# Value products of 64 columns placed before 64-column low products, and a head's first scores joined with the last head's smallest transposes

## The chip, the cores and the metric

The kernel runs on one core of a Trainium2 chip. The metric is the device time of one execution in microseconds. Of the kernel before there are three timed runs: median 1168.77 us, 1167.53 to 1171.01. A profiled execution gives the trace, from which all durations below are taken.

## The reference

Attention with a decay from the cumulated logarithm of gates, causal, over 8 batches of 8 heads with 576 tokens and 64 values a head; then a feed-forward layer with softplus over all 4608 tokens.

```python
scores = scale * np.matmul(q, k.transpose(0, 1, 3, 2))
cum = np.cumsum(np.log(np.clip(f, 0.0001, 1.0)), axis=-1)
decay = cum[:, :, :, None] - cum[:, :, None, :]
scores = np.where(causal, -1000000000.0, scores + decay)
attn = np.exp(scores - np.max(scores, axis=-1, keepdims=True))
attn = attn / (np.sum(attn, axis=-1, keepdims=True) + 1e-09)
x = np.matmul(attn, v)            # heads put side by side: 4608 x 512
h = x @ w_in                      # 512 -> 2048
g = np.maximum(h, 0.0) + np.log1p(np.exp(-np.abs(h)))
out = g @ w_out                   # 2048 -> 512
```

## The kernel before

Products are made in a rounded 32-bit format whose operands are split into a high and a low part: `x` becomes `xh` and `xl`, and a product is the sum of high times high, low times high and high times low. So most matrices appear twice in the code, with h and l at the end of their names.

*Jobs.* Batch 0 is cut into smaller jobs, made without the split (`plain`). The other 56 heads are "whole" heads: jobs made by `whole`, worked by the functions inside `attention`. A whole head has five query tiles: 64 queries, then four times 128. Each tile's scores against all keys up to its end are two products into one PSUM bank (`scores`, lines 799 and 800); the last tile, 576 keys wide, takes two banks. VectorE adds the mask and takes the row minimum (line 804), ScalarE makes the exponential with the row sum (line 832). When all tiles of the head are done, `finish_stats` makes reciprocals, and each tile is scaled by them (line 862 or 860, on POOL, VectorE or ScalarE).

*Transposes.* `weights(bi)` transposes the scaled weights of four "banks" of keys into PSUM (`turn`, line 927), and splits them into high (line 216, a copying helper, or 946) and low (949). Bank 0 is the small one: the first 64 keys for the first 64 queries, and the last 64 keys for the last 64 queries. It has 64 rows only, so high and low lie one above the other in one tile `ph`, and one product takes both. Its transposes have 64 stationary columns. Banks 1 to 3 are 512, 448 and 320 + 192 columns wide.

*Values.* `output(gi)` (line 1060) multiplies: the stationary operand is `vhl`, the high and low values of a chunk of keys side by side, 2 x 64 = 128 columns; the moving one is `ph` or `pl`. The upper 64 rows of the result are what the high values give, the lower 64 what the low values give; `shift` copies one half to `x`, `put` (line 1086) adds the other. Group 0 is the first 64 queries, one product of 64 columns. Group 1 is the other 512 queries: 512 columns high and low, the other 64-column product, 448 high and low, 320 high and low, 192 high and low. Each group has a PSUM bank of its own.

*Feed-forward.* Blocks of 512 tokens: products up (line 1210, twelve for each 128 of the 2048), gate, products down (line 1295). Their units are dealt out between the units of the heads, so that TensorE has them to do while a head waits.

*Order.* The program's text makes no order of its own. Every step is an `Op` with its engines' estimated costs, the steps it comes after and the PSUM or SBUF buffers that it takes (`takes`); `Plan.run` plays these through and gives out, at each point, the step that could start first, ties by its place in the list. The engines' instruction streams are what comes out. A step that takes PSUM banks of tag "att" (four banks) must be first in that tag's queue; a `loose` step may pass others if one more bank than it needs is free. Scores are loose. `on_pe` is the estimate of a product: 0.444 ns a moving column, but no less than 0.92 ns a stationary column, so 0.12 us for 64 columns against 128.

*The loop over jobs* (line 1549 and what follows) makes the list: for job n the scores of head n (`s_`) and the transposes and value products of head n - 1 (`w_`, `o_`), as: tiles 0, 1, 2; banks 0 and 1; tile 3; bank 2; group 0 of the output; bank 3; preparation of the next head; tile 4; group 1; `finish_stats`.

Of the kernel before, what the change touches and what calls it, by code (L numbers as in the profile page):

```python
# [157 lines left out]
def on_pe(n, times=1, m=128):  # L158

    return On("PE", times * (max(n * 0.000444, m * 0.00092) + 0.002))  # L160
# [7 lines left out]
def on_turn(n):  # L168

    return On("PE", 0.109 * n)  # L170
# [49 lines left out]
def tile_decay_attention_softplus_ffn(  # L220
# [18 lines left out]
    B, D, H, _, S = qkT.shape  # L239
# [20 lines left out]
                x32=2, wl=2, vhl=3, vraw=1, raw=2, one=2)  # L260
    plan = Plan(BUFS | dict(T0=4, stat=4, p=2, xh0=1, xh1=1, xl0=1))
    add, give = plan.add, plan.give

    def add_dma(emit, kb, n=1, eng="SP", **more):
        return add(on_dma(kb, n, eng), emit, lag=dma_lag(kb, n, eng), **more)
# [6 lines left out]
    def bank(tag, name):  # L272
        return psum.tile([P, 512], F32, tag=tag, name=name, bufs=BUFS[tag])
# [12 lines left out]
    T = {}  # L286
# [321 lines left out]
    def attention(job):  # L608
# [161 lines left out]
            st["T"] = [a, q0_]  # L770


        def stat_tile(ti):
            q0, n_q, k0, pi, po = tiles[ti]
            end = q0 + n_q
            if ti == 0:
                st["p"] = add(NO_ENGINE, mark, takes=("p",), lag=0.0)
            m1, s1 = nm[0:n_q, ti : ti + 1], ls[0:n_q, ti : ti + 1]
            m0, s0 = nm[0:n_q, 5:6], lp[0:n_q, 4:5]
            if end - k0 <= 512:  # L780
                pieces = [(k0, end, s1)]
            else:
                mid = (k0 + end) // 2
                pieces = [(k0, mid, s0), (mid, end, s1)]
            todo, mins = [], []
            for i, (a, z, acc) in enumerate(pieces):
                box = {}
                final = z == end

                def scores(e, box=box, a=a, z=z):  # L790
                    o = bank("att", f"s{n}_{ti}_{a}")[:, 0 : z - a]
                    box["o"] = o[0:n_q]
                    if plain:
                        e.matmul(  # L794
                            o, part32(0, q0, q0 + P), part32(1, a, z), start=True, stop=not quad,
                        )
                        return
                    o = box["o"]
                    e.matmul(o, qA[:, q0:end], kA[:, a:z], start=True, stop=False)  # L799
                    e.matmul(o, qB[0:ST, q0:end], kB[0:ST, a:z], start=False, stop=True)  # L800

                def row_min(e, box=box, w=z - a, i=i, final=final):
                    right = MW - P + n_q if final else w
                    e.tensor_tensor_reduce(  # L804
                        out=box["o"], in0=box["o"], in1=cmask[0:n_q, right - w : right],
                        scale=-0.125, scalar=m0 if i else 3.0e38, op0=ALU.add, op1=ALU.min,
                        accum_out=m1 if final else m0,
                    )

                def sums(e, box=box, h=heads[ti % len(heads)]):  # L810
                    c, (plus, minus) = cum[0][:, 0:P], (x[:, h : h + 1].to_broadcast([BH, P]) for x in eye8)
                    e.matmul(box["o"], c, plus, start=False, stop=False)
                    e.matmul(box["o"], minus, c, start=False, stop=True)

                on = on_pe32(z - a) if plain else on_pe(z - a, 2)
                o = add(on, scores, after=st["T"], takes=("att",), loose=True)
                if quad:
                    o = add(on_pe32(2 * P), sums, after=[o, decay_ready["quad"]] + eye8_set)
                    cum_used.append(o)
                m = add(  # L820
                    On("DVE", 0.076 + (z - a) / 960), row_min, lag=0.2, after=[o] + mask_set + stat_set,
                    takes=("stat",) if ti == 0 and i == 0 else (),
                )
                st.setdefault("scores", []).append(o)
                st.setdefault("min", []).append(m)
                mins.append(m)
                todo.append((a, z, acc, box))
            for a, z, acc, box in todo:

                def weight(e, a=a, z=z, box=box, acc=acc):  # L830
                    o = pt[pi][0:n_q, po + a - k0 : po + z - k0]
                    e.activation(o, box["o"], AF.Exp, bias=m1, scale=-1.0, accum_out=acc)  # L832

                x = add(on_act(z - a, 0.19, True), weight, after=mins + [st["p"], ps_set[number % 2, pi]])
                give("att", [x])
                st.setdefault("sum", []).append(x)
                st.setdefault("exp", {}).setdefault(ti, []).append(x)
# [31 lines left out]
        used = {i: [] for i in range(len(banks))}  # L869
        tags = {}  # L870

        def weights(bi):
            spans, w = [], 0
            for key, lo, hi, vi, vc in banks[bi]:
                spans.append((key, lo, hi, (vi, vc), w))
# [73 lines left out]
                e.tensor_sub(box["l"], box["ps"][:, 0:w], box["h"].bitcast(F32))  # L949

            need = list(dict.fromkeys(need)) + halves_set
            m = add(on_turn(len(blocks) - 0.48 * small + len(sums)), turn, after=need, takes=("att",))
            for _ in spread_:
                give("one", [m])
            st.setdefault("turned", []).append(m)
# [87 lines left out]
            for bi, ops in used.items():  # L1043
                give(tags[bi], ops)

        def output(gi):
            g0, g1, h, tok = groups[gi]
            g, j = h // 2, h % 2
            todo = sorted(
                (p for p in parts if p[0] < g1 and p[1] > g0), key=lambda p: (max(p[0], g0) > g0, p[2])  # L1050
            )
            box, last = {}, []
            for i, (lo, hi, bi, vc, at, pbox, ready, small) in enumerate(todo):
                a, z = max(lo, g0), min(hi, g1)

                def values(e, i=i, a=a, z=z, vc=vc, o=at + a - lo, pbox=pbox, xs="h" if small else "hl"):
                    if i == 0:
                        box["ps"] = bank("att", f"o{n}_{gi}")
                    for x in xs:
                        e.matmul(  # L1060
                            box["ps"][:, a - g0 : z - g0], st["vhl"][:, vc[1], :],
                            pbox[x][:, o : o + z - a],
                            start=i == 0 and x == "h", stop=i == len(todo) - 1 and x == xs[-1],
                        )

                on = on_pe(z - a, len("h" if small else "hl"))
                op = add(
                    on, values, after=ready + last + st["V"],
                    takes=("att",) if i == 0 else (),
                )  # L1070
                last = [op]
                used[bi].append(op)
            st.setdefault("ends", []).extend(last)
            w = g1 - g0


            def to():
                if b not in x_of:
                    x_of[b] = buf("x32", [P, NCC, S], f"x32_{b}")
                return x_of[b][64 * j : 64 * j + 64, g, tok : tok + w]  # L1080

            def shift(e):
                copy(e, to(), box["ps"][64 - 64 * j : 128 - 64 * j, 0:w])

            def put(e):
                e.tensor_add(to(), box["ps"][64 * j : 64 * j + 64, 0:w], to())

            needs = last + x_taken.get(b, [])
            takes = () if b in x_taken else ("x32",)
            c = add(on_act(w, psum=True), shift, after=needs, takes=takes)  # L1090
            d = add(on_dve(w), put, after=[c])
            x_taken.setdefault(b, [c])
            puts = [d]
            wrote.setdefault(b, []).append((tok, tok + w, d))
            give("att", puts)
            if gi == len(groups) - 1:
                give("T", st["scores"])
                give("vhl", st["ends"])
                for bi, ops in used.items():
                    if banks[bi][0][:3] == (0, 0, 64):  # L1100
                        give("ph64", ops)
                    else:
                        give("ph", ops)
                        give("pl", ops)

        def loads():
            if quad:
# [7 lines left out]

        return dict(
            load=loads, prepare=None if plain else prepare, fin=finish_stats,
            s=[lambda ti=ti: stat_tile(ti) for ti in range(nt)],
            w=[lambda bi=bi: weights(bi) for bi in range(len(banks))],
            o=[output_tiled] if plain else [lambda gi=gi: output(gi) for gi in range(len(groups))],  # L1120
        )


# [414 lines left out]
    for n in range(len(jobs) + 1):  # L1538
# [10 lines left out]
        s_, w_, o_ = list(cur["s"]), list(old["w"]), list(old["o"])  # L1549
        units = s_[:-2] if len(s_) > 3 else s_[:1]  # L1550
        s_ = s_[len(units) :]
        if w_:
            for i, u in enumerate(w_[:-1]):
                units.append(u)
                if i == 1 and s_:
                    units.append(s_.pop(0))
            if len(o_) > 1:
                units.append(o_.pop(0))
            units.append(w_[-1])
# [68 lines left out]
```

## Time and profile before

| | |
|---|---|
| median of three runs | 1168.77 us |
| the profiled execution's own time | 1169.16 us |
| its span, from first to last instruction | 1167.4 us |
| products on TensorE | 6236 |
| first and last scores of a whole head | 113.0 and 959.4 us |
| DMA, share of 16 engines | 54% |

In rows of the trace, PE is TensorE's products and PEld its loads of stationary operands, which run beside products; DVE is VectorE, ACT ScalarE, POOL GpSimd. `o<-ph,vhl 128*128 128x64` reads: tile `o` is written from `ph` and `vhl`, the stationary operand has 128 rows and 128 columns, the moving one 128 rows and 64 columns. In grouped rows stand the busy time, the mean length of one in ns, then the engine's idle time just before and who ended it. In rows in order of time stand start and length in us. Ends of products are modelled, so recorded products overlap; what a product costs TensorE is read from start to start.

### The profile page before, as it was taken

How to read it: one execution, taken by the hardware profiler on the slowest of the kernel's cores; microseconds unless marked ns; L12 is line 12 of the kernel's file. 1: busy time of each engine (PE TensorE's matmuls, PEld its weight loads, DVE VectorE, ACT ScalarE, POOL GpSimd, SP SyncE). 2: the span in 40 equal slices, each digit the busy share in tenths (PEclk: the TensorE clock that was granted, in tenths of full speed). 3: DMA queues.
4: the chain of work that ended last, by engine and by line, in shares of the span. 5: the costliest groups of instructions: out<-in, count | busy, mean ns of one | idle time of the engine just before them, and what ended most of it. 6: DMA issues, size and time to landing. Idle time of an engine off the chain costs nothing.

```text
span 1167.4 us, 19457 instructions
## 1 busy us (share of the span) xinstructions
PE 1153.1 (99%) x6236; PEld 958.0 (82%) x6236; DVE 799.1 (68%) x1986; ACT 834.1 (71%) x1987; POOL 146.1 (13%) x158
## 2 busy tenths in 40 slices
PE   8999999999999999999999999999999999999998
PEld 6776788888888888888888888888888888888887
DVE  7889999877776778667877777677866772223322
ACT  6887788978867877678767786787867873444543
POOL 3424221100111101011011001110011100000000
PEclk9999999999999999999999999999999999999999
DMA  8867776555666546656566557654666433211211
GB/s 240 245 211 212 193 187 164 144 153 164 160 195 183 155 133 199 180 156 170 152 173 185 161 152 202 175 153 141 188 169 185 121 110 124 75 54 37 90 55 37
DMA packets 118758, 180.36 MB, mean 155 GB/s; under 512 B 20784, under 2 KB 78416, under 8 KB 118656
## 3 DMA queue, kind: packets, MB, share of 16 engines
q1 hardware_dynamic: 118488, 178.97, 53.7%
q8 instruction: 50, 0.82, 0.3%
q14 instruction: 52, 0.43, 0.1%
q10 hardware_dynamic: 168, 0.15, 0.0%
HBM read 109.98 MB, written 35.95 MB: 125 GB/s over the span
## 4 chain that ended last, share of the span: by engine, by line
PE 85%; DVE 8%; DMA 3%; ACT 2%; issue 1%; SPq 0%; POOL 0%; DVEq 0%; ACTq 0%; POOLq 0%
PE acc L1295 30%; PE h L1210 30%; PE b L927 7%; PE o L1060 6%; PE s L800 3%; PE s L799 3%; DMA T<-T 2%; PE h L1191 1%; DVE s L804 1%; PE s L794 1%; PE acc L1314 1%; ACT p L832 1%; DMA wl<-wil_d 1%; DVE xl L1162 1%; DVE pl L949 1%
## 5 line engine op out<-in xcount | busy, mean ns | idle before, releaser
L1210 PE MATMUL h<-xh,wih 128*128 128x512 f32 (+1 forms) x576 | 230.4, 403 | 0.0
L832 ACT ACTIVATE p<-s,negm 128x288 f32<-128x288 f32 (+7 forms) x384 | 183.6, 481 | 57.2 <-DVE negm L804 52.4
L1210 PE MATMUL h<-xl,wih 128*128 128x512 f32 (+1 forms) x576 | 216.6, 379 | 0.0
L804 DVE CUSTOM_DVE_ANT_0 s<-s,cmask 128x288 f32<-128x288 f32 (+6 forms) x320 | 137.9, 440 | 88.5 <-PE s L800 83.4
L862 POOL TENSOR_SCALAR p<-p,rsum 128x448 f32<-128x448 f32 (+4 forms) x89 | 98.8, 1119 | 744.1 <-DVE rsum L846 390.0
L1257 DVE SCALAR_TENSOR_TENSOR h<-h,e 128x512 f32<-128x512 f32 x136 | 95.8, 705 | 130.5 <-ACT e L1249 129.4
L1243 ACT ACTIVATE e<-h 128x512 f32<-128x512 f32 x144 | 85.9, 597 | 118.2 <-PE h L1210 117.1
L1295 PE MATMUL acc<-woh_dt_float32r,gh 128*128 128x512 f32 x376 | 152.8, 406 | 0.0
L1210 PE MATMUL h<-xh,wl 128*128 128x512 f32 (+1 forms) x576 | 148.8, 380 | 0.0
L1295 PE MATMUL acc<-woh_dt_float32r,gl 128*128 128x512 f32 x376 | 147.2, 391 | 0.0
L1295 PE MATMUL acc<-wol_dt_float32r,gh 128*128 128x512 f32 x376 | 147.0, 391 | 0.0
L949 DVE TENSOR_TENSOR pl<-b,ph 128x512 fp32r<-128x512 f32 x168 | 111.1, 666 | 32.2 <-ACT ph L216 28.9
L216 ACT CAST ph<-b 128x512 fp32r<-128x512 f32 (+2 forms) x178 | 85.3, 483 | 58.2 <-PE b L927 52.6
L1210 PEld LDWEIGHTS h<-xh,wl 128*128 128x128 f32 x576 | 104.8, 188 | 21.6
L927 PE MATMUL b<-ident,p 128*128 128x128 f32 (+1 forms) x728 | 118.8, 269 | 2.5 <-ACT p L832 1.2
L1265 DVE TENSOR_TENSOR gl<-h,gh 128x512 fp32r<-128x512 f32 x136 | 93.6, 688 | 40.4 <-ACT gh L216 39.9
L1210 PEld LDWEIGHTS h<-xh,wih 128*128 128x128 f32 x576 | 108.7, 189 | 15.2 <-issue 0.2
L1210 PEld LDWEIGHTS h<-xl,wih 128*128 128x128 f32 x576 | 108.9, 189 | 14.4 <-DVE xl L1162 0.2
L927 PEld LDWEIGHTS b<-ident,p 128*128 128x128 f32 (+1 forms) x728 | 86.6, 138 | 18.3 <-ACT p L832 3.9
L216 ACT CAST gh<-h 128x512 fp32r<-128x512 f32 x114 | 67.0, 588 | 46.9 <-DVE h L1257 43.3
L799 PE MATMUL s<-T 128*64 128x64 f32 x336 | 98.0, 303 | 0.9 <-ACT p L832 0.6
L800 PE MATMUL s<-T 68*64 68x64 f32 x336 | 97.7, 295 | 0.0
(166 smaller groups left out, 2218.9 us busy)
## 6 DMA issues: line engine op xcount, KB each, us to landing
wl<-wil_d SPq DMA_DIRECT2D x72, 512.0 KB
T<-T SPq DMA_DIRECT2D x224, 144.0 KB
raw<-in_qkT SPq DMA_DIRECT2D x112, 144.0 KB
g_d<-gh SPq DMA_DIRECT2D x84, 128.0 KB
g_d<-gl SPq DMA_DIRECT2D x84, 128.0 KB
vr<-in_vR SPq DMA_DIRECT2D x64, 160.0 KB
out<-ob SPq DMA_DIRECT2D x35, 256.0 KB
sto<-in_w_out SPq DMA_DIRECT2D x11, 512.0 KB
```

The lines of the kernel that those rows point to most:

```text
L216: (e.tensor_copy if hasattr(e, "tensor_copy") else e.copy)(out, in_)
L799: e.matmul(o, qA[:, q0:end], kA[:, a:z], start=True, stop=False)
L800: e.matmul(o, qB[0:ST, q0:end], kB[0:ST, a:z], start=False, stop=True)
L804: e.tensor_tensor_reduce(out=box["o"], in0=box["o"], in1=cmask[0:n_q, right - w : right], scale=-0.125, scalar=m0 if i else 3.0e38, op0=AL ...
L832: e.activation(o, box["o"], AF.Exp, bias=m1, scale=-1.0, accum_out=acc)
L862: e.tensor_scalar(a, a, f_, None, ALU.mult)
L927: e.transpose(box["ps"][0 : x.shape[1], at : at + one.shape[1]], x, one)
L949: e.tensor_sub(box["l"], box["ps"][:, 0:w], box["h"].bitcast(F32))
L1210: e.matmul(o, l, r, start=m == 0, stop=m == 11)
L1257: e.scalar_tensor_tensor(h, h, 0.0, box["e"], ALU.max, ALU.add)
L1265: e.tensor_sub(box["l"], box["t"], box["h"].bitcast(F32))
L1295: e.matmul(st["acc", tt], l, r[fc], start=first and m == 0, stop=last and m == 2,)
```

## The change

The two groups of the output become one chain. `output()` goes through the four wide parts of group 1 (512, 448, 320, 192 columns), each high and then low. Between the high and the low product of the second part it puts the 64-column product of group 0, between those of the third part the 64-column product of group 1. The low product behind a 64-column one then has only the high values as its stationary operand, 64 columns (`m`), and writes only the upper 64 rows: low weights times low values are left out there. The other two low products keep 128 columns. The chain takes group 1's bank with its first step and group 0's with its second, and stands where group 1 stood; `finish` holds the shift and the addition as before, group 0 first.

`joined` and `join` put several steps' instructions into one `Op` with the sum of their costs and all that they come after. For whole heads with a whole head before them, tile 0's scores (two products of 64 columns) and bank 0's transposes become such a joined item: it stands after tiles 1 and 2 where bank 0 stood, takes two PSUM banks at once, and isn't loose. The buffers that tile 0 took for the head are taken by whichever tile comes first.

```diff
+    def join(op, cost, emit, after):
+        op.parts.append(emit)
+        op.on = [On("PE", op.on[0].cost + cost)]
+        for d in after:
+            if d not in op.after and d is not op:
+                op.after.append(d)
+                d.users.append(op)
+                op.missing += 1
+        return op
...
-                o = add(on, scores, after=st["T"], takes=("att",), loose=True)
+                if into:
+                    o = join(into, 0.106, scores, st["T"])
+                else:
+                    o = add(on, scores, after=st["T"], takes=("att",), loose=True)
...
+            if into:
+                m = join(into, 0.164, turn, need)
+            else:
+                m = add(on_turn(len(blocks) - 0.48 * small + len(sums)), turn, after=need, takes=("att",))
...
+            wide = sorted((x for x in todo if not x[-1]), key=lambda x: x[1])
+            narrow = sorted((x for x in todo if x[-1]), key=lambda x: x[0])
+            last, done = [], {}
+            for i, part in enumerate(wide):
+                mine = [part] + narrow[i - 1 : i] * (0 < i <= len(narrow))
+                fresh = [x[0] for x in mine if x[0] not in done]
...
+                    def product(x, which, m=2 * D):
+                        gi, a, z, _, c, o, pbox, *_ = x
                         e.matmul(
+                            boxes[gi]["ps"][0:m, a:z], st["vhl"][:, c, 0:m], pbox[which][:, o : o + z - a],
...
+                    for x in mine:
+                        product(x, "h")
+                    product(mine[0], "l", D if len(mine) > 1 else 2 * D)
...
+                    On("PE", on_pe(w, 2).cost + 0.054 * (len(mine) - 1)), values,
+                    after=list(dict.fromkeys(r for x in mine for r in x[7])) + last + st["V"],
+                    takes=("att",) * len(fresh),
...
+        if nplain < n < len(jobs):
+
+            def row(s=units.pop(0), w=w_[0]):
+                op = joined()
+                s(op)
+                w(op)
+                op.takes = "att", "att"
+                plan.queue["att"].append(op)
+
+            w_[0] = row
```

More of the change, by code (lines that the diff above doesn't have):

```diff
@@ L262, in tile_decay_attention_softplus_ffn, with joined, row @@
     add, give = plan.add, plan.give
+    def joined():
+        parts = []
+        def row(e):
+            for part in parts:
+                part(e)
+        op = add(On("PE", 0.0), row)
+        op.parts = parts
+        return op
[7 more added lines that the diff above has]
+                op.missing += 1
+        return op
     def add_dma(emit, kb, n=1, eng="SP", **more):
@@ L770, in prepare, with stat_tile @@
             st["T"] = [a, q0_]
-        def stat_tile(ti):
+        def stat_tile(ti, into=None):
             q0, n_q, k0, pi, po = tiles[ti]
             end = q0 + n_q
-            if ti == 0:
+            if "p" not in st:
                 st["p"] = add(NO_ENGINE, mark, takes=("p",), lag=0.0)
@@ L821, in stat_tile @@
                     On("DVE", 0.076 + (z - a) / 960), row_min, lag=0.2, after=[o] + mask_set + stat_set,
-                    takes=("stat",) if ti == 0 and i == 0 else (),
+                    takes=() if "stat" in st else ("stat",),
                 )
+                st["stat"] = True
                 st.setdefault("scores", []).append(o)
@@ L870, in attention, with weights @@
         tags = {}
-        def weights(bi):
+        def weights(bi, into=None):
             spans, w = [], 0
@@ L951, in weights @@
             need = list(dict.fromkeys(need)) + halves_set
-            m = add(on_turn(len(blocks) - 0.48 * small + len(sums)), turn, after=need, takes=("att",))
+            if into:
+                m = join(into, 0.164, turn, need)
+            else:
+                m = add(on_turn(len(blocks) - 0.48 * small + len(sums)), turn, after=need, takes=("att",))
             for _ in spread_:
@@ L1044, in output_tiled, with output, values @@
                 give(tags[bi], ops)
[L1046 to L1059, printed above, removed]
+        def output():
+            boxes = [{} for _ in groups]
+            todo = []
+            for gi, (g0, g1, *_) in enumerate(groups):
+                for lo, hi, bi, vc, at, pbox, ready, small in parts:
+                    a, z = max(lo, g0), min(hi, g1)
+                    if a < z:
+                        todo.append((gi, a - g0, z - g0, bi, vc[1], at + a - lo, pbox, ready, small))
+            wide = sorted((x for x in todo if not x[-1]), key=lambda x: x[1])
[4 more added lines that the diff above has]
+                fresh = [x[0] for x in mine if x[0] not in done]
+                def values(e, i=i, mine=mine, fresh=fresh):
+                    for gi in fresh:
+                        boxes[gi]["ps"] = bank("att", f"o{n}_{gi}")
+                    def product(x, which, m=2 * D):
+                        gi, a, z, _, c, o, pbox, *_ = x
@@ L1060, in values @@
                         e.matmul(
-                            box["ps"][:, a - g0 : z - g0], st["vhl"][:, vc[1], :],
-                            pbox[x][:, o : o + z - a],
-                            start=i == 0 and x == "h", stop=i == len(todo) - 1 and x == xs[-1],
-                        )
-                on = on_pe(z - a, len("h" if small else "hl"))
+                            boxes[gi]["ps"][0:m, a:z], st["vhl"][:, c, 0:m], pbox[which][:, o : o + z - a],
+                            start=gi in fresh and which == "h",
@@ L1067, in output @@
+                            stop=gi == 0 or (i == len(wide) - 1 and which == "l"),
+                        )
+                    for x in mine:
+                        product(x, "h")
+                    product(mine[0], "l", D if len(mine) > 1 else 2 * D)
+                w = part[2] - part[1]
                 op = add(
-                    on, values, after=ready + last + st["V"],
-                    takes=("att",) if i == 0 else (),
+                    On("PE", on_pe(w, 2).cost + 0.054 * (len(mine) - 1)), values,
+                    after=list(dict.fromkeys(r for x in mine for r in x[7])) + last + st["V"],
+                    takes=("att",) * len(fresh),
@@ L1070, in output @@
                 )
                 last = [op]
-                used[bi].append(op)
-            st.setdefault("ends", []).extend(last)
-            w = g1 - g0
+                for x in mine:
+                    used[x[3]].append(op)
+                    done[x[0]] = [op]
+            for gi, (g0, g1, h, tok) in enumerate(groups):
+                finish(gi, h // 2, h % 2, g1 - g0, tok, boxes[gi], done[gi])
+            give("T", st["scores"])
+            give("vhl", last)
+            for bi, ops in used.items():
+                if banks[bi][0][:3] == (0, 0, 64):
+                    give("ph64", ops)
+                else:
+                    give("ph", ops)
+                    give("pl", ops)
@@ L1077, in to, with finish @@
+        def finish(gi, g, j, w, tok, box, ended):
             def to():
@@ L1086, in put @@
                 e.tensor_add(to(), box["ps"][64 * j : 64 * j + 64, 0:w], to())
-            needs = last + x_taken.get(b, [])
+            needs = ended + x_taken.get(b, [])
             takes = () if b in x_taken else ("x32",)
@@ L1092, in output @@
             x_taken.setdefault(b, [c])
-            puts = [d]
             wrote.setdefault(b, []).append((tok, tok + w, d))
[L1095 to L1104, printed above, removed]
+            give("att", [d])
         def loads():
@@ L1117, in attention @@
             load=loads, prepare=None if plain else prepare, fin=finish_stats,
-            s=[lambda ti=ti: stat_tile(ti) for ti in range(nt)],
-            w=[lambda bi=bi: weights(bi) for bi in range(len(banks))],
-            o=[output_tiled] if plain else [lambda gi=gi: output(gi) for gi in range(len(groups))],
+            s=[lambda into=None, ti=ti: stat_tile(ti, into) for ti in range(nt)],
+            w=[lambda into=None, bi=bi: weights(bi, into) for bi in range(len(banks))],
+            o=[output_tiled if plain else output],
         )
```

## The prediction

> **What bounds the kernel now.** I read the first page from the top: engines' busy time, then the span in 40 slices.
>
> ```profile
> span 1167.4 us, 19457 instructions
> PE 1153.1 (99%) x6236; PEld 958.0 (82%) x6236; DVE 799.1 (68%) x1986; ACT 834.1 (71%) x1987; POOL 146.1 (13%) x158
> PEclk9999999999999999999999999999999999999999
> ```
>
> TensorE is busy for 99% of the span at the full granted clock; the next engine, ScalarE, has 71%. An average can hide stages, so I asked for the stretches that this kernel has: before the first full head (113 us is where the first product of line 799 starts), the heads with the weight preparation beside them, the heads with the feed-forward blocks, and the end without heads. Each row is start:end, length, then busy time by engine.
>
> ```profile
> 0.00:113.00 113.00, 107.35 (x713) 77.75 (x713) 94.52 (x263) 91.67 (x216) 44.82 (x66) 1.00 0.77 230
> 113.00:240.00 127.00, 123.03 (x780) 103.31 (x780) 115.32 (x313) 108.00 (x286) 23.91 (x20) 1.00 0.64 168
> 240.00:950.00 710.00, 709.66 (x3786) 600.76 (x3785) 521.82 (x1302) 537.25 (x1315) 76.44 (x71) 1.00 0.59 166
> 950.00:1167.40 217.40, 213.01 (x963) 176.13 (x961) 67.43 (x111) 97.17 (x171) 0.87 (x1) 1.00 0.22 69
> ```
>
> The first figure after the length is TensorE: 709.66 of 710 us from 240 to 950, but only 123.03 of 127 from 113 to 240. The view of waits for 240 to 1000 us says the same: one row, which is all there is.
>
> ```profile
> PE o L1060 <- DVE x L1086: 0.8, 2, 0.6
> ```
>
> So in this stage nothing is worth anything except TensorE's own time, and there every nanosecond of it counts. From 113 to 240 us TensorE also waits for others; these are its longest waits there.
>
> ```profile
> PE b L927 <- POOL p L862: 1.1, 2, 0.9
> PE b L927 <- ACT p L832: 1.0, 1, 1.0
> ```
>
> **How TensorE's time is made up.** The recorded length of a matmul (0.39 us at 512 columns) is not what it costs; its cost is the distance between starts, 0.23 us. The small items are therefore priced by start-to-start distances between undisturbed neighbours. First the smallest score tile (lines 799 and 800), then the two smallest transposes (line 927), each in front of a feed-forward product:
>
> ```profile
> 386.76 0.39 PE L1210 MATMUL h<-xl,wih 128*128 128x512 f32 x1
> 386.99 0.19 PE L799 MATMUL s<-T 128*64 128x64 f32 x1
> 387.02 0.22 PE L800 MATMUL s<-T 68*64 68x64 f32 x1
> 387.08 0.48 PE L1210 MATMUL h<-xh,wih 128*128 128x512 f32 x1
> 387.39 0.39 PE L1210 MATMUL h<-xl,wih 128*128 128x512 f32 x1
> ...
> 407.59 0.31 PE L800 MATMUL s<-T 68*128 68x320 f32 x1
> 407.74 0.22 PE L927 MATMUL b<-ident,p 68*64 68x68 f32 x1
> 407.80 0.27 PE L927 MATMUL b<-halves,p 128*64 128x128 f32 x1
> 407.83 0.48 PE L1210 MATMUL h<-xh,wih 128*128 128x512 f32 x1
> 408.14 0.40 PE L1210 MATMUL h<-xl,wih 128*128 128x512 f32 x1
> ```
>
> From 386.76 to 387.39 are 0.63 us for two products of 0.23 and the score pair: the pair costs 0.17. From 407.59 to 408.14 are 0.55 for one of 0.23, one 320 wide of 0.15 (407.59 to 407.74) and the two transposes: 0.17 again. Now the 64-column value products of line 1060, one standing alone among feed-forward products, one in the chain of value products (the row with x2 holds the 64-wide one and the 448-wide one):
>
> ```profile
> 505.83 0.40 PE L1295 MATMUL acc<-woh_dt_float32r,gl 128*128 128x512 f32 x1
> 506.06 0.19 PE L1060 MATMUL o<-ph,vhl 128*128 128x64 f32 x1
> 506.09 0.48 PE L1210 MATMUL h<-xh,wih 128*128 128x512 f32 x1
> 506.41 0.39 PE L1210 MATMUL h<-xl,wih 128*128 128x512 f32 x1
> ...
> 577.23 0.40 PE L1060 MATMUL o<-pl,vhl 128*128 128x512 f32 x1
> 577.46 0.48 PE L1060 MATMUL o<-ph,vhl 128*128 128x64 f32 x2
> 577.78 0.37 PE L1060 MATMUL o<-pl,vhl 128*128 128x448 f32 x1
> 577.99 0.30 PE L1060 MATMUL o<-ph,vhl 128*128 128x320 f32 x1
> ```
>
> Alone: 506.41 - 505.83 = 0.58, less 0.46 = 0.12 us. In the chain: 577.78 - 577.23 = 0.55, less 0.23 and less 0.21 for the 448-wide one (577.78 to 577.99) = 0.11. Yet a 64-wide product moves on after 0.03 (506.06 to 506.09). The other 0.08 shows as the lengthened 0.48 of the next product: its stationary operand cannot be loaded behind a product of 0.03 us, while behind one of 0.23 it can. What such an exposed load costs depends on the columns loaded, by the load records grouped by shape:
>
> ```profile
> L1060 PEld LDWEIGHTS o<-ph,vhl 128*128 128x128 f32 x336 | 63.3, 189 | 11.2 <-DVE x L1086 1.7 <-ACT ph L216 0.6 <-DVE ph L946 0.4
> L800 PEld LDWEIGHTS s<-T 68*64 68x64 f32 x56 | 7.5, 134 | 4.5 <-issue 0.3
> ```
>
> 128 columns are recorded with 189 ns, 64 columns with 134: 55 ns less. The score pair bears it out: its two products cost 0.17 together, the second is followed by a 128-column load (0.115, as the lone value product), so the first, followed by a 64-column load, costs 0.055 to 0.06.
>
> **The change part by part.** (1) Value products. Each head keeps its ten products, but each of the two 64-wide ones now stands directly in front of a low product (448 and 320 wide) that loads 64 stationary columns instead of 128. Cost of the 64-wide one before 0.115, after 0.06: 0.055 saved, twice a head. The load of the 64-wide product itself hides behind the 448-wide or 320-wide high product, as today's hide behind 0.23; the load after the low product hides behind its 0.21 or 0.15. The low products still stream 448 and 320 columns, so I cost them as before. What is dropped (low weights times low values in those two) frees no time of its own.
>
> (2) Joined item. Before: 0.17 + 0.17 = 0.34. After: four small products in a row, three followed by 64-column loads (3 x 0.06; the transposes' own step is 407.80 - 407.74 = 0.06) and one by a 128-column load (0.115): 0.295. Saved about 0.05, taken as 0.055, the difference of one load, for 55 heads (the first full head has no full head before it). A change from scores to transposes costs nothing visible: 407.59 to 407.74 is that neighbourhood, at 0.15 for 320 columns.
>
> (3) What is moved. The smallest score tile goes behind the next two tiles, with its row minimum on VectorE and its exponential on ScalarE; group 0 of the output goes from between the last transposes to the chain at the end, with its shift on ScalarE and its addition on VectorE. No DMA and nothing of SP's or POOL's queue is moved. These are 64 columns wide (217 + 123, 307 + 193, 208 and 218 ns in the rows here), come no oftener than before, and both engines have a quarter of the middle stretch free (521.82 and 537.25 of 710): no cost on the path.
>
> ```profile
> L804 DVE CUSTOM_DVE_ANT_0 s<-s,cmask 64x64 f32<-64x64 f32 x56 | 12.2, 217 | 3.4 <-PE s L800 3.0
> L804 DVE DVE_READ_ACCUMULATOR2_ANT negm<- 64x1 f32 x64 | 7.9, 123 | 0.2
> L832 ACT ACTIVATE p<-s,negm 64x64 f32<-64x64 f32 x56 | 17.2, 307 | 7.5 <-DVE negm L804 5.9
> L832 ACT ACTIVATION_READ_ACCUMULATOR p<-s,negm 64x1 f32 x64 | 12.3, 193 | 0.0
> L216 ACT COPY x<-o 64x64 f32<-64x64 f32 x56 | 11.7, 208 | 3.5 <-PE o L1060 2.2
> L1086 DVE TENSOR_TENSOR x<-o,x 64x64 f32<-64x64 f32 x56 | 12.2, 218 | 6.4 <-ACT x L216 5.8
> ```
>
> (4) The added wait. The joined item needs the scores' operands, the last head's normalised weights and two free PSUM banks at once. Behind it on TensorE's queue stands everything. The transposes had the long part of that wait already; what is new is that the scores wait with them, and nobody needs these early: the head's sums are closed only after its last tile. The planner fills with feed-forward products until all is ready. Taken as 0; bounds: nothing, and 0.55 us per head (the mean of the two waits for POOL above) if the filling fails.
>
> **The sum.** From 240 us on there are 93 of the 112 64-wide products and 45 joined items, from 113 to 240 us 19 and 10:
>
> ```profile
> L1060 PE MATMUL o<-ph,vhl 128*128 128x64 f32 x93 | 18.3, 197 | 0.0
> L799 PE MATMUL s<-T 128*64 128x64 f32 x45 | 8.7, 193 | 0.1
> ```
>
> (93 + 45) x 0.055 = 7.6 us, all on the path. The early 29 x 0.055 = 1.6; there TensorE also waits for others, part of what it saves becomes waiting, and I count half: 0.8. Together 8.4 us. After the last head TensorE has only feed-forward products, which start earlier by what was saved and end earlier by as much; the end past the last product stays. The profiled execution took 1169.16 us (span 1167.4) and becomes 1160.8; it lay 0.39 over the median of the runs, so the median goes from 1168.77 to **1160.4 us**, 0.7% faster. Two numbers are chosen: half in the early stretch (ends 0 and 1.6), and the 64-column load in the middle of an accumulation priced as that of the scores (ends: no shorter than 128 columns, and 0.055 shorter).
>
> **The rivals.**
> *The array empties when the number of columns changes.* If a switch between 128 and 64 stationary columns let the running product drain, each would cost what a 64-wide product still runs after it has moved on, 0.19 - 0.03 = 0.16 us (506.06). There are four new switches a head: 224 x 0.16 = 35.8 us, so 1168.8 - 2.7 (joined items alone) + 35.8 = about 1202; from 8.4 / 224 = 0.037 us a switch on, it is slower. Against it: the score pair at 386.99 holds two such switches, and its 0.17 is used up by two loads. Chance 0.02. [...]
> *TensorE stands at the joined item.* If each stood 0.55 us, 55 x 0.55 = 30 us, so about 1190; if half did, 1168.8 - 8.4 + 15 = 1175.4. From 0.15 us a head it is slower than before. For it: the item now needs two banks and heads the bank queue, so all later tiles wait behind it; the early stretch has such waits. Against it: from 240 us on TensorE waits twice in all, and the transposes waited for the same data. Chance 0.04.
> *The change doesn't do what it says:* the shortened load brings nothing among the value products, since the row that shows it is from the scores. Then only the joined items remain, 45 x 0.055 and half of 10 x 0.055: 2.8 us, 1166.0. Chance 0.07.
> *The new plan costs or gives something of its own.* The planner's costs change (a 64-wide product from 0.12 to 0.054), so all engines' orders are drawn again. The room for that is TensorE's 4.0 idle us of 113 to 240: doubled, 1164.4; gone, 1156.4. Chance 0.07 each for more than 3 us of loss (1163.4 to 1168) and of gain (below 1157.4).
>
> **How the numbers follow.** Forecast with small variations (1157.4 to 1163.4) 0.73; gain from the plan 0.07; loss by the plan 0.07; no shorter load 0.07; the two slower cases 0.06. 0.3% (3.5 us) is about what a measurement of this kernel can tell from no change: below 1165.3 lie 0.73 + 0.07 + two thirds of the loss, 0.85; within, the rest of the loss, the unshortened load and a mild form of the stall, 0.10; slower 0.05. The range goes from 1157.0 to 1165.5; what is left out is most of the plan's gain, the upper third of its loss, the unshortened load and the slower cases, about 0.2.
>
> **What the next profile would show.** Right: 64-wide value products all inside the value chain, the low product after each with a load of 64 columns near 134 ns, and from the 448-wide high product's start to the 320-wide one's about 0.48 us (0.21 + 0.06 + 0.21); scores and small transposes in one row of four, about 0.30; TensorE's waits after 240 us still about 1 us. Wrong: load records of these low products near 189 ns, a lengthened low product of over 0.1 us, or waits at line 927 or 799 for POOL, ScalarE or a bank in many heads.

## The result, and the profile after

Twenty runs of each kernel: before 1167.78 us median, changed 1159.86 us. The ratio is 0.9934, 95% interval 0.992 to 0.9948: 0.66% or some 7.9 us faster, where 1160.4 us and 0.7% were forecast. The profiled execution of the changed kernel took 1158.51 us, 1.35 under its median, while that of the kernel before lay 1.4 over its own; so the two profiles lie 10.7 us apart, 2.7 more than the medians. In three of the experiments below one run of 1376 us or more is left out of the median.

The page's first rows:

```profile
span 1156.7 us, 19558 instructions
PE 1142.6 (99%) x6236; PEld 952.1 (82%) x6236; DVE 781.0 (68%) x1992; ACT 834.0 (72%) x1981; POOL 147.3 (13%) x158
```

Two of the stretches in the same cuts as before (start:end, length, busy time by engine, TensorE first):

```profile
113.00:240.00 127.00, 123.63 (x800) 105.78 (x799) 118.11 (x321) 108.89 (x295) 20.20 (x19) 1.00 0.64 175
240.00:950.00 710.00, 708.83 (x3821) 601.31 (x3820) 510.88 (x1320) 543.70 (x1319) 82.88 (x73) 1.00 0.58 166
```

As many products on TensorE as before (x6236), and from 240 to 950 us TensorE is as full as before, but 3821 products begin or end in that stretch instead of 3786. The waits from 240 to 1000 us are still few, though not the same ones: score tiles now wait for ScalarE.

```profile
PE s L820 <- ACT p L857: 1.1, 4, 0.4
PE acc L1336 <- DVE gl L1306: 0.5, 1, 0.5
```

The joined item, then the value chain, in order of time (start, length). In the chain the rows with x2 hold a wide high product and the 64-column product behind it.

```profile
382.57 0.84 PE L1251 MATMUL h<-xh,wl 128*128 128x512 f32 x3
383.25 0.19 PE L820 MATMUL s<-T 128*64 128x64 f32 x1
383.28 0.22 PE L821 MATMUL s<-T 68*64 68x64 f32 x1
383.34 0.25 PE L952 MATMUL b<-ident,p 68*64 68x68 f32 x1
383.43 0.27 PE L952 MATMUL b<-halves,p 128*64 128x128 f32 x1
383.45 0.47 PE L1336 MATMUL acc<-woh_dt_float32r,gh 128*128 128x512 f32 x1
383.77 0.39 PE L1336 MATMUL acc<-wol_dt_float32r,gh 128*128 128x512 f32 x1
...
580.42 0.40 PE L1095 MATMUL o<-ph,vhl 128*128 128x448 f32 x2
580.65 0.40 PE L1095 MATMUL o<-pl,vhl 128*64 128x448 f32 x1
580.89 0.34 PE L1095 MATMUL o<-ph,vhl 128*128 128x320 f32 x2
581.07 0.34 PE L1095 MATMUL o<-pl,vhl 128*64 128x320 f32 x1
581.24 0.25 PE L1095 MATMUL o<-ph,vhl 128*128 128x192 f32 x1
```

From 383.25 to 383.77 are 0.52 us for the four small products and one feed-forward product of 0.23: the joined item costs 0.29, where 0.295 was forecast and 0.34 was paid before. It holds from place to place: at 35 joined items after 240 us that stand in front of feed-forward products, the same distance gives a median of 0.285 us, with 0.172 for the score pair and 0.175 for the transposes in the trace of before. From 580.42 to 580.89 are 0.47 for 448 high, 64, 448 low: 0.48 was forecast, and 0.466 is the median of 46 such places. The load records, grouped by shape, show why:

```profile
L1095 PEld LDWEIGHTS o<-pl,vhl 128*128 128x128 f32 x112 | 21.1, 188 | 1.1
L1095 PEld LDWEIGHTS o<-pl,vhl 128*64 128x64 f32 x112 | 15.0, 134 | 0.6
```

The 112 low products behind a 64-column one load 64 columns in 134 ns, the other 112 load 128 in 188.

### The profile page after: what moved, and what is told of

Same layout as the page of the kernel before. It is cut to its first block, busy times and chain, and to the rows that moved or that the text cites. A ratio compares the mean times of both kernels' runs of the same rounds, so it can differ in the third digit from the quotient of the medians.

```text
span 1156.7 us, 19558 instructions
## 1 busy us (share of the span) xinstructions
PE 1142.6 (99%) x6236; PEld 952.1 (82%) x6236; DVE 781.0 (68%) x1992; ACT 834.0 (72%) x1981; POOL 147.3 (13%) x158
## 4 chain that ended last, share of the span: by engine, by line
PE 82%; DVE 8%; ACT 4%; DMA 3%; issue 1%; SPq 1%; POOL 0%; DVEq 0%; ACTq 0%; POOLq 0%
PE h L1251 30%; PE acc L1336 30%; PE b L952 7%; PE o L1095 6%; PE s L820 3%; PE s L821 3%; DMA sto<-in_w_out 2%; ACT p L857 1%; DVE s L825 1%; DMA T<-T 1%; PE acc L1355 1%; DVE pl L974 1%; DVE wil L541 1%; DVE woh_dt_float L495 1%; DVE xl L1203 1%
## 5 line engine op out<-in xcount | busy, mean ns | idle before, releaser
L1251 PE MATMUL h<-xh,wih 128*128 128x512 f32 (+1 forms) x576 | 223.9, 391 | 0.0
L887 POOL TENSOR_SCALAR p<-p,rsum 64x64 f32<-64x64 f32 (+4 forms) x89 | 102.3, 1158 | 730.3 <-DVE rsum L871 291.9
L1298 DVE SCALAR_TENSOR_TENSOR h<-h,e 128x512 f32<-128x512 f32 x136 | 95.8, 704 | 143.7 <-ACT e L1290 142.9
L216 ACT CAST gh<-h 128x512 fp32r<-128x512 f32 x134 | 78.6, 587 | 72.4 <-DVE h L1298 65.5
L820 PE MATMUL s<-T 128*128 128x192 f32 (+1 forms) x336 | 101.1, 306 | 4.0 <-ACT p L857 3.1
L216 ACT CAST ph<-b 128x512 fp32r<-128x512 f32 (+2 forms) x146 | 76.1, 526 | 39.3 <-PE b L952 38.8
L821 PE MATMUL s<-T 68*128 68x192 f32 (+1 forms) x336 | 98.1, 296 | 0.0
## 6 DMA issues: line engine op xcount, KB each, us to landing
T<-T SPq DMA_DIRECT2D x224, 144.0 KB
raw<-in_qkT SPq DMA_DIRECT2D x112, 144.0 KB
```

Of the source, the lines that this page charges most:

```text
L216: (e.tensor_copy if hasattr(e, "tensor_copy") else e.copy)(out, in_)
L887: e.tensor_scalar(a, a, f_, None, ALU.mult)
L1251: e.matmul(o, l, r, start=m == 0, stop=m == 11)
L1298: e.scalar_tensor_tensor(h, h, 0.0, box["e"], ALU.max, ALU.add)
```

## The experiments

To separate what TensorE has to do from when it may do it, I estimated for each trace what its sequence of split products and transposes costs, by a rule of mine that is itself an estimate from these rows: each product starts when the one before has streamed, or when its own load is done, whichever is later, and a load starts when the product before starts and the load before is done. Streaming, from start-to-start distances: 0.228 us for 512 columns, 0.2005 for 448, 0.1465 for 320, 0.135 for 288, 0.1185 for 256, 0.088 for 192, 0.03 for 64 and 68; the 0.054 for 128 is an estimate that no distance shows, and as no load is held to be shorter it moves no start. Loads, from the distances between starts of the split products' loads that follow one another at once (0.108 to 0.114 us behind one of 128 columns, 0.055 to 0.058 behind one of 64 in the trace of before): 0.112 for 128 columns (0.109 in transposes), 0.057 for 64. This "work" is no time that a run shows; it is a sum by which runs are compared. The "rest" is the profiled span less this work: the unsplit jobs at the start, the end, and all waiting. It comes from one execution, and these lie up to 2.5 us off their medians; the last column moves it to the median of the runs.

| kernel | ratio to before (95%) | work | profiled span | rest | rest at the median |
|---|---|---|---|---|---|
| before | 1 | 1023.4 | 1167.4 | 144.0 | 142.6 |
| changed | 0.9934 (0.992-0.9948) | 1014.7 | 1156.7 | 142.0 | 143.4 |
| changed, low products load 128 | 0.9961 (0.9949-0.9974) | 1020.8 | 1161.1 | 140.3 | 141.0 |
| value chain alone | 0.9993 (0.9976-1.001) | 1017.2 | 1168.1 | 150.9 | 149.6 |
| joined item alone | 1.0035 (1.0022-1.0047) | 1020.7 | 1169.1 | 148.4 | 150.3 |
| changed, three low products load 64 | 0.9922 (0.99-0.9943) | 1014.7 | 1158.4 | 143.7 | 143.1 |
| changed, 10 us more work, early | 0.9994 (0.9973-1.0015) | 1024.7 | 1165.6 | 140.9 | 140.9 |
| changed, 10 us more work, middle | 1.0021 (0.9993-1.0049) | 1024.7 | 1167.7 | 143.0 | 143.0 |
| changed, transposes before the 512-wide low product | 1.0009 (0.9987-1.003) | 1011.3 | 1169.3 | 158.0 | 156.7 |
| before, second plan | 0.9991 (0.9966-1.0016) | 1023.6 | 1169.2 | 145.6 | 143.2 |
| changed, second plan | 0.9937 (0.9909-0.9966) | 1014.7 | 1159.3 | 144.6 | 144.7 |
| joined item alone, second plan | 1.0006 (0.9978-1.0035) | 1020.8 | 1167.4 | 146.6 | 147.0 |
| value chain alone, second plan | 0.9979 (0.9956-1.0001) | 1017.5 | 1165.5 | 148.0 | 148.1 |
| changed, planner's old prices | 0.9969 (0.9955-0.9984) | 1014.6 | 1162.6 | 148.0 | 148.0 |

**The shorter load by itself.**

```diff
-                    product(mine[0], "l", D if len(mine) > 1 else 2 * D)
+                    product(mine[0], "l")
```

> The changed kernel, its order and plan untouched, but the two low products behind the 64-column ones load 128 stationary columns again. If the shorter load is the gain (my theory): about 0.05 us comes back at 112 places, 5.9 us, so about 1165.8 us where the changed kernel has 1159.9 and the kernel before 1167.8; the load records of these products go from about 134 to 189 ns. If the new place of the products or the new plan is the gain: stays at 1159.9. If a switch of the number of columns drains the array: as fast as the changed kernel or faster.

1163.55 us, ratio 0.9961. The plan is the same, so only the loads differ: the records of all 224 low products are now 188 ns, as this row of that run shows.

```profile
L1095 PEld LDWEIGHTS o<-pl,vhl 128*128 128x128 f32 x224 | 42.1, 188 | 1.8
```

The work rises by 6.1 us, as expected, the time by 3.7 us from median to median, by 3.2 going by the two ratios, and the span by 4.4. So the shorter load is a real part of the gain, but not every nanosecond of it arrives: the rest at the median fell by 2.4 us. Neither the new place alone nor a drain explains this run.

**Each half alone.** The value chain without the joined item (`if nplain < n < len(jobs):` becomes `if False:`), and the joined item with the output functions of the kernel before.

> The new value chain without the joined item. Theory: the joined item's share goes, 55 x 0.06 = 3.3 us, so about 1163.2 us. If the joined item stalls TensorE or is worth nothing: 1160 or less.

> The joined item with the value products of the kernel before. Theory: 3.3 us off the kernel before, about 1164.5 us. If the joined item costs waits of its own: 1167.8 or more. With the value chain alone the two gains should add up to that of the whole change, within 2 us; if they do not, the new plan has a part.

Both theories failed, and the gains do not add up to that of the whole change; of the other cases on record only the joined item's own waits (1167.8 or more) came about. The chain alone took 1168.62 us, no faster than before; the joined item alone 1172.9, slower. Yet their work is 6.2 and 2.7 us below that of the kernel before, and 6.2 + 2.7 is the 8.7 of the whole change within 0.2. The work adds up; the rest doesn't: 149.6 and 150.3 at the median, where the kernel before has 142.6. In the run with the joined item alone, one place is seen at once. In order of time, with the idle time before a row and who ended it in brackets:

```profile
222.82 0.40 PE L820 MATMUL s<-T 128*128 128x288 f32 x1 [0.45 <-ACT p L857]
...
225.13 0.32 PE L820 MATMUL s<-T 128*64 128x64 f32 x1 [1.12 <-ACT p L857]
225.26 0.29 PE L821 MATMUL s<-T 68*64 68x64 f32 x1
225.74 0.32 PE L952 MATMUL b<-ident,p 68*64 68x68 f32 x1 [0.19 <-ACT p L857]
```

The stretches around it (the granted clock is the third figure from the end):

```profile
220.90:224.30 3.40, 2.51 (x13) 1.48 (x11) 3.17 (x12) 3.35 (x11) 1.08 (x1) 1.00 0.65 167
224.30:231.10 6.80, 5.62 (x22) 4.62 (x23) 6.59 (x16) 5.36 (x17) 0.00 (x0) 0.50 0.39 100
231.10:234.50 3.40, 3.40 (x19) 2.96 (x18) 2.25 (x7) 2.40 (x5) 1.84 (x1) 0.99 0.27 58
```

The joined item at 225.13 stands 1.12 us for an exponential of ScalarE, with nothing of the feed-forward layer in front of it; and from 224.3 to 231.1 the granted clock is half. The timed runs of this kernel show a mean granted clock of 0.996 or 0.997, those of the changed kernel mostly 1.0. That is the rival "TensorE stands at the joined item", seen at one of 55 items in a kernel that has the item but not the chain; it is a part of what this kernel lost, not all of it.

**A switch of the number of columns.**

```diff
-                    product(mine[0], "l", D if len(mine) > 1 else 2 * D)
+                    product(mine[0], "l", D if i < len(wide) - 1 else 2 * D)
```

Low weights times low values are left out in three of the four low products. A kernel that leaves them out in all four was planned too (1.1 us less was expected) and has no measured time.

> The changed kernel with the first low product of the chain (512 wide) at 64 stationary columns too, so that three of the four leave out low weights times low values. Two more switches between 128 and 64 columns a head, same order. Theory (a switch costs nothing, that load was hidden): as the changed kernel, ratio to the kernel before 0.993. If a switch drains the array (0.16 us): 112 x 0.16 = 18 us more, ratio 1.009.

Ratio 0.9922 and 1159.62 us, as the changed kernel (0.9934, 1159.86) within both intervals, where a drain of 0.16 us a switch would have given 1.009. 112 more switches between 64 and 128 stationary columns cost nothing that can be measured here: no drain.

**How much of TensorE's work counts, and where.** In 11 whole heads, four further 512-wide products into the bank that the first real one overwrites:

```diff
+                    if i == 0 and nplain <= number < nplain + 11:
+                        for _ in range(4):
+                            product(mine[0], "h", alone=True)
                     for x in mine:
                         product(x, "h")
```

> The changed kernel, same order and plan, with four additional 512-wide value products (4 x 0.23 us, overwritten, no effect on the output) in each of the first 11 whole heads: 10.1 us more work for TensorE before about 250 us. It measures how much of TensorE's work counts in the early stretch. Prediction's choice of half: +5 us, about 1165; if all counts: +10, about 1170; if the early stretch is set by others: +0 to 2.

> The same 10.1 us of additional work in 11 heads of the middle (the 17th to the 27th whole head, about 350 to 520 us). Theory: all of it counts, +10 us, about 1170, ratio 1.002. If the middle has hidden slack: less than +8.

Medians 1167.43 and 1169.45 us: 7.6 and 9.6 us over the changed kernel, spans 8.9 and 11.0 over. Going by the ratios it is 7.0 and 10.2 us. In the middle all counts, as claimed, within an interval of some 4 us either way. In the early stretch it is about three quarters, more than the half that I had chosen; but the interval there is some 3 us either way, so neither the half nor a difference between early and middle is settled.

**One step more of the same kind.** The transposes of bank 3 between the first high and low product of the chain, that low product with 64 columns, both in one item with two banks; scores may then pass it only if two banks stay free:

```diff
+            def tail_(w=w_[-1], o=o_[0]):
+                op = joined()
+                op.takes = "att", "att"
+                plan.queue["att"].append(op)
+                w(op)
+                o(op)
+
+            o_ = [tail_]
...
+                    into.parts.insert(0, high)
+                    op = join(into, on_pe(w, 2).cost, low, part[7] + st["V"])
```

> A further step of the same kind: the transposes of bank 3 stand between the first high and the first low product of the chain (512 wide), and that low product loads 64 columns. One more exposed 128-column load a head becomes a 64-column one: 56 x 0.055 = 3.1 us less work, ratio 0.991 if the plan lets it through; other orders of the plan may take it back, as the runs with one half of the change did.

The work fell by 3.4 us more, as meant, and the kernel took 1169.79 us, 10 more than the changed one. The longest of its waits from 240 to 1000 us (total, times, longest), where line 1096 holds the chain and line 858 the exponential:

```profile
PE o L1096 <- ACT p L858: 4.7, 5, 1.2
```

One of the five places in order of time:

```profile
578.41 0.37 PE L1096 MATMUL o<-ph,vhl 128*128 128x448 f32 x1
579.55 0.30 PE L1096 MATMUL o<-ph,vhl 128*128 128x64 f32 x1 [0.78 <-ACT p L858]
```

Five times, once a batch, group 0's product stands in mid-chain for the bank of a score tile whose exponential isn't done. That is 4.7 of the 16 us by which the rest rose over the changed kernel (13 at the median). What the others are, the waits do not show; this run, too, has a clock below 1 (0.997), with half the clock for 6.8 us from 225.9 us on.

**The same work in another order.** One number of the planner that no hardware sees, the time after which a freed buffer counts as free:

```diff
-PELAG, GLAG, PORTLAG = 0.1, 0.2, 0.09
+PELAG, GLAG, PORTLAG = 0.1, 0.21, 0.09
```

> The kernel before with one number of the planner changed that no hardware sees (a freed buffer is held to be seen after 0.21 instead of 0.20 us). Same instructions, another order. Theory that the order alone moves the time by several us: differs from 1167.8 by up to 5 us either way. Rival: within 1 us.

> The changed kernel with the same 0.21. TensorE's work stays 8.7 us below that of the kernel before whatever the order; time between 1156 and 1165 if the order has several us of its own, 1159.9 within 1 us if not.

> The joined item alone (third run) with 0.21. If its slowness came from the order (a wait of 1.1 us at a joined item and 6.8 us at half clock, near 225 us): back to 1163 to 1168. If joining itself costs: 1172 again.

> The value chain alone (second run) with 0.21. Its work is 6.2 us below the kernel before. If the order took that gain: another time than 1168.6, between 1160 and 1170; if the chain has a cost that belongs to it: 1168.6 again.

Before and changed kernel came out as with their first plans (1168.59 and 1161.21 us, ratios 0.9991 and 0.9937): for these two, several us by the order alone did not show, and the gain of the change is there in a second plan. The joined item alone lost most of its slowness (1169.67, ratio 1.0006), the chain alone gained a little (1167.39, 0.9979), less than the two intervals can tell apart; both rests at the median fell, by 3.3 and 1.5 us, but stayed over that of the kernel before. So a part of what the joined item lost is an accident of one order. What else the halves lost is there in both plans tried; whether it belongs to them, and what it is, these runs don't settle. TensorE's waits in the profile, summed from 113 to 1000 us, are a part of it for the joined item (10.0 us with the first plan, 7.2 with the second; before 4.6 and 6.8), but hardly for the chain (6.8 and 6.2).

**The planner's old prices.** Same instructions, joined scores held to cost 0.24 and a 64-wide value product 0.12 us:

```diff
-                    o = join(into, 0.106, scores, st["T"])
+                    o = join(into, 0.24, scores, st["T"])
...
-                    On("PE", on_pe(w, 2).cost + 0.054 * (len(mine) - 1)), values,
+                    On("PE", on_pe(w, 2).cost + 0.12 * (len(mine) - 1)), values,
```

> The changed kernel, same instructions, but the planner holds the joined scores to cost 0.24 us and a 64-wide value product 0.12 us, as before the change. If the new prices are part of the gain: slower than 1160 by more than 2 us; if only TensorE's work counts: 1160 within 2 us.

1164.71 us, ratio 0.9969: about half of the gain gone with the work unchanged (1014.6). In its trace TensorE's waits from 240 to 1000 us add up to 2.9 us, where the changed kernel has 1.6; the longest stands before transposes:

```profile
717.91 0.66 PE L952 MATMUL b<-ident,p 128*128 128x128 f32 x4 [1.02 <-DVE ph L971]
```

So the plan with the new prices, which are close to what the rows show (0.055 to 0.06 for such a product), is some 4 us better: ratio 0.9969 against 0.9934. That the prices do it, and not an accident of this one order, is likely but not shown: the second plan with the new prices kept the gain (0.9937), while the old prices were tried with one plan only.

## Why the prediction was right, point by point

*TensorE's time is what counts.* Right for the middle: 10 us more work there made the kernel 9.6 us slower by the medians, 11.0 by the spans.

*An exposed load of 64 columns costs 0.055 us less than one of 128.* Right: 134 against 188 ns in the records, 0.47 us in the chain (0.48 forecast), 0.29 for the joined item (0.295 forecast). Switching only this back cost 3.2 to 3.7 us of a work difference of 6.1, where I counted 5.6 us for these loads: in time they brought less than forecast.

*The sum.* 167 places at 0.055 us are 9.2 us of work; the sequences give 8.7 (1023.4 to 1014.7). I let 8.4 arrive, 7.9 did.

*Half in the early stretch.* Probably too low: about three quarters of added early work arrived. On the 1.6 us of early savings this is 0.4 us.

*The joined item waits at no cost.* Right for the changed kernel: its only waits from 240 to 1000 us are the two rows above, 1.6 us in all, and the four for ScalarE stand before score tiles of 192 columns, none at a joined item. It isn't a property of the item: alone, one stood 1.12 us with a half clock around it.

*The rivals.* The drain is out (three low products with 64 columns: ratio 0.9922, where 1.009 was to be expected of a drain). That the shortened load brings nothing is out (the first run). The stall is out for this kernel, but showed at one item of another one. The rival that I priced too low is the new plan: I gave it 4 us of room and a chance of 0.07 on each side. With the work given, the rest at the median ranged from 140.9 to 156.7 us over the kernels above; the plan with the old prices took 4 us, and each half of the change lost nearly its whole gain or more. The forecast of 1160.4 was right because the work was summed rightly and because, in this plan, the rest stayed within 1 us of that of the kernel before (143.4 and 142.6 at the median; in the two profiled executions it was 2 us lower). The first was argued. The second was not; a second plan bears it out, but ahead of the result it was luck.

## What to carry to other kernels

The products with 64 moving columns, 0.03 us from start to start, hid hardly any of the load behind them here: they cost 0.115 us in front of a load of 128 columns and 0.055 to 0.06 in front of one of 64. So put narrow products in front of the ones that load the fewest stationary columns, or one behind the other, so that a long load follows only once. In a kernel whose order is drawn by a planner, sum the engine's work from the sequence first and compare it with the time: a gain in work of under one per cent can be taken back whole by the new order, and prices in the planner that fit the trace are likely a part of the gain. Try each part of such a change alone only with that sum at hand; the times of the halves here would have spoken against both.

## What the runs showed of the hardware that was not expected

In three runs the clock fell to half with no wait of TensorE's over 1.3 us nearby. In the run with the joined item alone TensorE was busy for 2.51 of the 3.40 us before 224.3, and its longest wait thereabouts was the 1.12 us that ended at 225.13; the half clock lasted 6.8 us. The run with transposes before the 512-wide low product shows it for the 6.8 us from 225.9 us on; its longest waits up to 240 us, apart from 2.1 us before its first product, are 1.3 and 1.0 us. The chain alone shows it once, after 1.59 of 3.40 us busy and waits of 0.9 and 1.0 us; columns as above, TensorE first, clock third from the end.

```profile
127.60:131.00 3.40, 1.59 (x7) 0.62 (x5) 3.37 (x8) 1.98 (x6) 2.12 (x2) 1.00 0.87 230
131.00:134.40 3.40, 3.33 (x8) 2.14 (x9) 3.19 (x10) 1.59 (x6) 0.00 (x0) 0.50 0.61 150
134.40:137.80 3.40, 3.40 (x20) 2.56 (x19) 2.32 (x7) 2.31 (x5) 0.00 (x0) 1.00 0.81 241
```

How thin the stretch was does not decide it by itself. In the run with the planner's old prices TensorE was busy for 1.60 of 3.40 us and stood 2.0 us in one piece, and the clock stayed whole (1.00 in the rows and as the mean of that execution):

```profile
129.90:133.30 3.40, 1.60 (x5) 0.94 (x6) 3.37 (x12) 2.16 (x7) 0.19 (x1) 1.00 0.74 214
133.30:136.70 3.40, 3.40 (x19) 2.04 (x18) 3.34 (x11) 2.37 (x9) 0.00 (x0) 1.00 0.20 57
```

What made the clock fall in the one run and not in the other, these runs leave open.
